# The tail of a cached-attention decode kernel: the last 224 rows of W_down on seven DMA engines, the output weights in three loads, two score buffers, masks on GpSimd

## The chip, the cores and the metric

The kernel runs on one core of one Trainium2 chip. The metric is the device time of one execution, in microseconds (us). A trace covers one execution. Its "span" runs from the first to the last instruction and is about 2 us shorter than the device time (658.7 against 660.76 us for the traced execution of the kernel before).

Engine names in the profile: PE is TensorE (PEld its weight loads), DVE is VectorE, ACT is ScalarE, POOL is GpSimd, SP is the engine that issues most DMAs. The core has 16 DMA engines, which all its queues share. An "instruction fetch" below is a packet that the trace marks as kind `instruction`; I read it as an engine fetching the next block of its program.

## The reference, cut to what matters

```python
# x: (2,1,512)   k_cache, v_cache: (2,32,8192,128)   wq: (512,4096)   wo: (4096,512)
# W_gate, W_up: (512,1376)   W_down: (1376,512)      all bfloat16
def _A_ref(x, k_cache, v_cache, wq, wo):            # one query token, 32 heads
    q = (x @ wq)...                                  # per head
    scores = einsum("bhqd,bhkd->bhqk", q, k) * Dh**-0.5
    o = softmax(scores) @ v
    return o.reshape(B, Sq, Hq*Dh) @ wo
def _B_ref(x, W_gate, W_up, W_down):
    gate = x @ W_gate ; up = x @ W_up
    return (relu(gate) * up) @ W_down
h  = x + _A_ref(layernorm(x), ...)
h2 = h + _B_ref(layernorm(h), ...)
```

K and V are 268 MB of the 281 MB that one execution reads. Four heads of one batch row are one step (8.4 MB of K and as much of V), so there are 16 steps.

## The kernel before: the parts that matter here

Every engine runs its own instruction list. A small helper records which operation wrote and read each named piece of data and emits the semaphore waits that this needs. VectorE multiplies K by the query and adds up (`products`, `sums`), ScalarE takes exponentials (`exps`), TensorE multiplies by V. One score buffer `sc` serves all steps, so the sum of step n waits until TensorE has finished step n-1:

```python
    def sums(n, lo, hi, key):
        red(sc[:, lo:hi], kt[n % 2][:, lo:hi, 0:8], AXIS.X, keys, [key])
    ...
    for n in range(L):
        if n:
            for k in ("sc", "pm"):
                s.last.pop(k, None)
                s.readers[k] = [v_done(n - 1)]
        scores(n, HALVES if n == 0 else (0, T))
```

At the end the weights come in on the SP queue in this order: `wo` (two loads of 2 MB), W_gate, W_up (three quarters, then one quarter), W_down (three loads, then the last 96 rows on 96 partitions):

```python
    for k in range(NGR):                                   # wo: 2 x 2 MB
        s.dma("sp", f"dwo{k}", ... writes=[f"wo{k}"], extra=[v_done(L - 1)])
    ...
    for f, r in blocks:                                    # W_down: 512, 512, 256 rows
        s.dma("sp", f"dwd{f}", ... writes=[f"wd{f}"], extra=x_free)
    s.dma("sp", "dwdl", lambda: sync.dma_start(out=wd_l, in_=B_W_down[FULL:F, :]),
          writes=["wdl"], extra=x_free)                    # the last 96 rows
```

and the tail computes

```python
    attention_rows(0, NK - JG, True)      # 16 matmuls with the first half of wo
    normalize(B - 1, NGR - 1)
    attention_rows(NK - JG, NK, False)    # 16 matmuls, wait for the whole second half
    # transpose on VectorE, layernorm, 12 gate matmuls, 12 up matmuls, product on VectorE (qrep),
    # columns of the product, 44 y matmuls, cast of y (sc), two output DMAs
```

The softmax here doesn't subtract the row's maximum and nothing guards it: scores larger than these inputs give would overflow.

## Time and profile before

| | before |
|---|---|
| time, median of 3 | 660.43 us (660.39 to 660.52) |
| span of the trace | 658.7 us |
| VectorE busy | 618.0 us, 94% |
| DMA, mean over the span | 427 GB/s, 281 MB read |
| VectorE waiting for K, in all | 4.6 us |

These are two rows of the page's second part, the span in 40 equal slices. The DMA row is the busy share of the 16 engines in tenths; the other is what they moved.

```profile
DMA  9999999999999999999999999999999999999996
GB/s 378 447 446 414 418 446 442 446 438 394 446 442 442 442 402 438 442 442 442 410 430 442 442 442 414 426 442 442 442 434 406 446 442 438 438 406 442 418 421 248
```

The DMA engines are busy from the first slice into the last one. The trace's packet records show the same from near: a packet of 65,536 bytes takes 2.42 us, and V arrives every 38.70 us, which is 16 such packets. So the length of the byte stream sets the time up to about 644 us. What can still change is how the last weights arrive and what is computed on them. This is the chain that ended last (start us, length us, what), in the kernel before:

```profile
621.36 22.94 DMA v<-in_A_wo_dram
644.29 0.14 issue
644.43 1.91 PE mm L596 x13
646.36 0.73 DVE osb L611
648.55 1.76 PE o L654 x12
650.72 1.85 PE mm L654 x12
652.66 0.69 DVE qrep L674
654.12 1.37 PE y L645 x44
655.51 0.29 DVE sc L711
```

The second load of `wo` lands at 644.29. Then come its matmuls, the transpose (osb), the gate matmuls (o), the up matmuls (mm), their product (qrep), the y matmuls and the cast. Nothing in this chain after 644.43 waits for a DMA.

The trace holds more: for each load, one landing time for each DMA engine that carried it. I sorted these and subtracted the start of the span. Each row of the next table is one load, and its 16 numbers are the 16 engines from first to last. The record does not say which engine a time belongs to.

```
kernel before, us            first 12 engines ............................................ 13th   14th   15th   last
wo, 2nd half  641.99 642.01 642.13 642.14 642.17 642.29 642.30 642.33 642.37 642.38 642.44 642.59 642.91 643.70 643.76 644.29
gate          645.30 645.32 645.44 645.45 645.48 645.60 645.61 645.65 645.68 645.69 645.76 645.89 646.23 647.00 647.08 647.61
up, 3/4       647.81 647.83 647.95 647.96 647.98 648.10 648.12 648.14 648.18 648.18 648.25 648.39 648.72 649.51 649.58 650.09
W_down, last  652.28 652.36 652.45 652.48 652.50 652.54 652.60 652.62 652.70 652.73 652.82 652.97 653.18 653.93 653.99 654.60
```

A load is usable when its last engine is done. Twelve engines finish within 0.6 us of each other, and four trail by up to 2.3 us. They fell back where instruction fetches came into the stream. The packet records show these: 16,384 bytes at 27.1 and 635.0 us, and 8,192 bytes at 177.2, 198.9 and 638.6 us. The loads that land between them show one step for each fetch.

### The profile page before, as it was taken

What the parts mean: (1) busy time and instruction counts of PE and PEld (TensorE: products, weight loads), DVE (VectorE), ACT (ScalarE), POOL (GpSimd) and SP (SyncE); (2) the same over time, 40 slices, a digit from 0 to 9 for tenths busy, and PEclk for the clock granted to TensorE, in tenths of its full rate; (3) what the DMA queues carried; (4) which work ended last, traced back from release to release, by engine and by line L of the source; (5) the groups of instructions that cost most, each with busy time, mean ns of one, the idle gap of its engine ahead of it and who ended that gap; (6) DMA issues with size and microseconds to landing.
All of it is one profiled execution on the core that took longest, in us unless ns stands there. A gap on an engine that the chain in (4) does not pass through costs nothing. (4 is left out here: it accounts for less than half of the span.)

```text
span 658.7 us, 3100 instructions
## 1 busy us (share of the span) xinstructions
PE 115.0 (17%) x1234; PEld 47.3 (7%) x1234; DVE 618.0 (94%) x184; ACT 59.4 (9%) x155; POOL 3.8 (1%) x15
## 2 busy tenths in 40 slices
PE   2200302003030110303011030300203030020365
PEld 1000100001010000101000010100001010010122
DVE  1799999999999999999999999999999999999972
ACT  2301010010101001010100101010010101001100
POOL 2000000000000000000000000000000000000000
PEclk9655655656565575656557565565756556575655
DMA  9999999999999999999999999999999999999996
GB/s 378 447 446 414 418 446 442 446 438 394 446 442 442 442 402 438 442 442 442 410 430 442 442 442 414 426 442 442 442 434 406 446 442 438 438 406 442 418 421 248
DMA packets 6474, 281.13 MB, mean 427 GB/s; under 512 B 738, under 2 KB 836, under 8 KB 1348
## 3 DMA queue, kind: packets, MB, share of 16 engines
q1 hardware_dynamic: 6456, 281.06, 98.9%
q8 instruction: 3, 0.05, 0.0%
q14 instruction: 3, 0.02, 0.0%
q10 hardware_dynamic: 12, 0.00, 0.0%
HBM read 281.05 MB, written 0.00 MB: 427 GB/s over the span
## 5 line engine op out<-in xcount | busy, mean ns | idle before, releaser
L364 DVE TENSOR_TENSOR k<-k,qrep 128x32768 bf16<-128x32768 bf16 (+3 forms) x18 | 275.9, 15327 | 4.6 <-DMA k<-in_A_k_cache_dram 4.6
L370 DVE TENSOR_TENSOR k<-k 128x4096 bf16<-128x4096 bf16 (+6 forms) x72 | 267.4, 3714 | 2.5
L406 PE MATMUL o<-v,pm 128*32 128x512 bf16 x960 | 83.9, 526 | 466.9 <-PEq L434 466.9
L383 ACT ACTIVATE pm<-sc 32x256 bf16<-32x256 f32 (+2 forms) x68 | 48.2, 709 | 562.9 <-DVE sc L227 562.1
L406 PEld LDWEIGHTS o<-v,pm 128*32 128x32 bf16 x960 | 35.2, 127 | 515.3 <-issue 508.4
L227 DVE TENSOR_REDUCE sc<-k 128x256 f32<-128x2048 bf16 (+2 forms) x17 | 36.7, 2160 | 0.8 <-PE o L406 0.3
L453 DVE TENSOR_REDUCE osb<-om 128x128 f32<-128x512 f32 x16 | 16.5, 1029 | 0.6
L383 ACT ACTIVATION_READ_ACCUMULATOR pm<-sc 32x1 f32 x68 | 15.8, 233 | 0.0
L349 DVE CAST qrep<-mm 32x512 bf16<-32x512 f32 x4 | 2.8, 696 | 11.1 <-PE mm L333 11.1
L449 DVE TENSOR_TENSOR om<-o,turn_of 128x512 f32<-128x512 f32 x16 | 10.9, 681 | 1.8 <-PE o L406 1.8
L413 PE MATMUL rep<-osb,spread 128*32 128x128 f32 x40 | 3.9, 420 | 48.4 <-DVE osb L453 45.0
L406 PE MATMUL o<-k,pm 128*32 128x512 bf16 x64 | 7.4, 628 | 7.7 <-ACT pm L383 5.3
L333 PE MATMUL mm<-v,om 128*64 128x512 bf16 x32 | 6.6, 572 | 8.7 <-DMA v<-in_A_wq_dram 8.5
L346 ACT ACTIVATE qrep<-mm 32x512 bf16<-32x512 f32 x12 | 7.0, 587 | 9.1 <-PE mm L333 8.9
L611 DVE STREAM_TRANSPOSE osb<-mm 128x512 f32<-128x512 f32 x1 | 0.7, 717 | 6.7 <-PE mm L596 6.7
L413 PEld LDWEIGHTS rep<-osb,spread 128*32 128x32 f32 x40 | 1.4, 146 | 50.9 <-DVE osb L453 46.6
L596 PE MATMUL mm<-v 128*2 128x512 bf16 x32 | 3.7, 620 | 3.0 <-DMA v<-in_A_wo_dram 3.0
L522 POOL TENSOR_TENSOR zm<-zm,zx 128x1 f32<-128x1 f32 x1 | 0.2, 191 | 627.5 <-ACT pm L383 627.5
L333 PEld LDWEIGHTS mm<-v,om 128*64 128x64 bf16 x32 | 2.5, 152 | 12.4 <-issue 10.3
L406 PEld LDWEIGHTS o<-k,pm 128*32 128x32 bf16 x64 | 2.0, 133 | 12.7 <-ACT pm L383 6.7
L301 DVE COPY xc<-st 128x8 f32<-128x8 f32 x1 | 0.2, 165 | 2.6 <-PE st L296 2.6
L654 PE MATMUL o<-k,sc 128*32 128x512 bf16 x12 | 1.9, 628 | 0.0
(81 smaller groups left out, 33.3 us busy)
## 6 DMA issues: line engine op xcount, KB each, us to landing
k<-in_A_k_cache_dram SPq DMA_DIRECT2D x2, 4096.0 KB, 26.8
v<-in_A_wq_dram SPq DMA_DIRECT2D x1, 4096.0 KB, 12.3
k<-in_A_v_cache_dram SPq DMA_DIRECT2D x1, 4096.0 KB, 31.4
v<-in_A_wo_dram SPq DMA_DIRECT2D x2, 2048.0 KB, 20.4
k<-in_A_v_cache_dram SPq DMA_DIRECT2D x1, 3072.0 KB, 38.3
k<-in_B_W_gate_dram SPq DMA_DIRECT2D x1, 1376.0 KB, 14.9
k<-in_B_W_up_dram SPq DMA_DIRECT2D x1, 1032.0 KB, 17.1
k<-in_A_v_cache_dram SPq DMA_DIRECT2D x1, 1024.0 KB, 40.4
```

Source lines behind the costliest of these rows:

```text
L227: s.op("dve", lambda: dve.tensor_reduce(out=out_, in_=in_, axis=axis, op=ALU.add), reads=reads, writes=writes)
L333: last = pe.matmul(out=ps[h * B * Q:(h + 1) * B * Q], lhsT=xnb[:, c].rearrange("p b q -> p (b q)"), rhs=wq_h[:, c, g:g + QP, h0 + h, :], s ...
L346: s.op("act", lambda src=src, dst=dst: act.activation(out=dst, in_=src, func=ACT.Copy), reads=[f"mm{t}"], writes=[key])
L349: s.op("dve", lambda src=src, dst=dst: dve.tensor_copy(dst, src), reads=[f"mm{t}"], writes=[key])
L364: s.op("dve", lambda: dve.tensor_tensor(out=kp, in0=kp, in1=_view(qrep[:, b, i, :], 0, [[0, hi - lo], [1, Dh]]), op=ALU.mult), reads=keys ...
L370: s.op("dve", lambda half=half, width=width: dve.tensor_tensor(out=kp[:, :, 0:half], in0=kp[:, :, 0:half], in1=kp[:, :, half:width], op=AL ...
L383: last = act.activation(out=p_of[ps, lo // TG:hi // TG, :, h], in_=sc[ps, lo:hi].rearrange("p (g t) -> p g t", t=TG), func=ACT.Exp, accum_ ...
L406: last = pe.matmul(out=o[g:g + W2], lhsT=pm[:, t // TG, :], rhs=vs[:, t:t + TG, :].rearrange("p t d -> p (t d)"), start=(t < P // Q * TG), ...
L413: return pe.matmul(out=rep_ps[u * Q:(u + 1) * Q, :], lhsT=spread.rearrange("k h m -> k (h m)"), rhs=osb[:, u, :], start=True, stop=True, s ...
L449: s.op("dve", lambda: dve.tensor_tensor(out=om.rearrange("p (t d) -> p t d", d=Dh), in0=o.rearrange("p (t d) -> p t d", d=Dh), in1=_view(t ...
L453: fn = lambda: dve.tensor_reduce(out=osb[:, u, :], in_=om.rearrange("p (t d) -> p d t", d=Dh), axis=AXIS.X, op=ALU.add)
L596: last = pe.matmul(out=ar_ps[g:g + B], lhsT=oc[:, k, :], rhs=wo_sb[:, k, :], start=False, stop=(k + P // Q >= NK), skip_group_check=True)
```

## The change

The intent: shift bytes of W_down from nine DMA engines to seven, so that the engines that end last have less to do; let half of the second `wo` matmuls run before the last of `wo` has landed; free VectorE's score sums from a wait; take three small mask reductions off VectorE. The diff, cut to its core (`...` marks cuts):

```diff
-    NF = F // P                      # 10 blocks of 128 rows, 96 rows left
+    NE = 7
+    NF = (F - 32 * NE) // P          # 9 blocks, 224 rows left
...
-    sc = sbuf("sc", (P, T), f32)
+    sc2 = [sbuf(f"sc{u}", (P, T), f32) for u in range(2)]
-    x_row = sbuf("x_row", (B, D), bf16)
+    x_row = osb.rearrange("p u d -> p (u d)")[0:B, 0:D // 2].bitcast(bf16)   # room; loaded again late
...
+        implied = [self.clock.get(t, {}) for t in out.items()]               # drop implied waits
+        out = {k: v for k, v in out.items() if all(c.get(k, 0) < v for c in implied)}
...
+    for h in range(G):               # three masks by GpSimd copies and memsets
+        s.op("pool", lambda q=q: pool.tensor_copy(eye_of[q], ident[q, q]), ...)
+        s.op("pool", ... pool.memset(head_blk[...]))
-        red(head_blk, ...)           # were three VectorE reductions
-        red(row_of[:, 0:B], ...)
-        red(eye_of, ...)
...
-            for k in ("sc", "pm"):
-                s.last.pop(k, None)
-                s.readers[k] = [v_done(n - 1)]
+            s.last.pop("pm", None)
+            s.readers["pm"] = [v_done(n - 1)]
...
-    for k in range(NGR):
+    WO = ((0, 0, JG), (1, 0, JG // 2), (1, JG // 2, JG))
+    for k, lo, hi in WO:             # wo: 2 MB, 1 MB, 1 MB
...
-    s.dma("sp", "dwdl", ... in_=B_W_down[FULL:F, :])
+    s.op("pool", lambda: pool.memset(X[0:Q, at:at + 4 * D], 0.0), writes=["wdl"], extra=x_free)
+    rest = B_W_down[FULL:F, :].rearrange("(h e i r) n -> h i e (r n)", h=2, e=NE, r=4)
+    for h in range(2):
+        for m in range(4):           # eight loads, seven partitions of 4 KB each
+            s.dma("act", f"dwl{h}{m}", lambda h=h, m=m: act.dma_start(
+                out=X[h * Q + m:h * Q + m + 4 * NE:4, at:at + 4 * D], in_=rest[h, m]), ...)
...
-    attention_rows(0, NK - JG, True)
     normalize(B - 1, NGR - 1)
-    attention_rows(NK - JG, NK, False)
+    for k, lo, hi in WO:
+        attention_rows(k * JG + lo, k * JG + hi, k == lo == 0)
...
-    s.op("pe", lambda: y_rows(act_t[0:LASTW, NF, :], wd_l, last=True), ...)      # 4 matmuls
+        for r in range(4):                                                       # 16 matmuls
+            last = y_rows(act_t[0:ML, NF + r, :], wd_l[:, r, :], last=(r == 3))
```

The cut leaves out one more edit: two of the four normalisations on VectorE are merged into one instruction.

There are 52 y matmuls instead of 44. The earlier blocks lose four with the tenth block, and the rest gains twelve.

More of the change, by code (lines that the diff above doesn't have):

```diff
@@ L69, in op @@
     def op(self, eng, fn, reads=(), writes=(), extra=(), gives=None, token=None):
+        if eng == "pool" and self.count[eng]:
+            extra = list(extra) + [(eng, self.count[eng])]
         waits = self.needs(eng, reads, writes, extra)
@@ L126 @@
     f32 = mybir.dt.float32
-    NF = F // P
-    FC = (F + P - 1) // P
+    NE = 7
+    NF = (F - 32 * NE) // P
+    FC = NF + 4
     FULL = NF * P
-    LASTW = F - FULL
+    ML = 32 + 4 * NE
     Q = P // G
@@ L149 @@
     assert Sq == 1 and Hkv == Hq and D == KC * P and Hq % (2 * G) == 0 and T % 32 == 0 and P == Dh
-    assert NQ % NS == 0 and P == 4 * Q and D == MT
+    assert F == FULL + 32 * NE and NQ % NS == 0 and P == 4 * Q and D == MT
     ctx.enter_context(tc.tile_critical(no_gpsimd_drain=True))
@@ L194 @@
     zi = late[:, NK + B * NQ:NK + B * NQ + B * NGR]
-    hd = sc[:, P // 2:P].bitcast(bf16).rearrange("p (c k b) -> p c k b", k=NR, b=B)
+    hd = sc2[0][:, P // 2:P].bitcast(bf16).rearrange("p (c k b) -> p c k b", k=NR, b=B)
     r2 = late[:, 2 * NK - 1:2 * NK]
+    x_late = vt.rearrange("p t d -> p (t d)")[0:B, NK * D + 4 * P:NK * D + 4 * P + D]
     act_t = late[:, 2 * NK:2 * NK + FC * B // 2].bitcast(bf16).rearrange("p (f b) -> p f b", b=B)
@@ L222 @@
     s.op("pool", lambda: pool.memset(pm, 0.0), writes=["pm"])
-    s.op("pool", lambda: pool.memset(osb, 0.0), writes=["osb"])
-    s.lists["pool"].append(((), lambda: pool.sem_inc(s.sem("o_in"), 1), None))
     def red(out_, in_, axis, reads, writes):
@@ L228, in red @@
              reads=reads, writes=writes)
+    for h in range(G):
+        q = slice(h * Q, (h + 1) * Q)
+        s.op("pool", lambda q=q: pool.tensor_copy(eye_of[q], ident[q, q]), reads=["ident"],
+             writes=["eye"])
+        s.op("pool", lambda h=h: pool.memset(head_blk[:, h:h + 1], 0.0), writes=[f"head{h}"])
+        s.op("pool", lambda h=h, q=q: pool.memset(head_blk[q, h:h + 1], 1.0),
+             writes=["head", f"head{h}"])
+    s.op("pool", lambda: pool.tensor_copy(row_of[:, 0:B], eye_of[:, 0:B]), reads=["eye"],
+         writes=["row_of"])
     def build_masks():
@@ L234, in build_masks @@
             i, ["lane"])
-        red(head_blk, ident.rearrange("p (h m) -> p h m", h=G), AXIS.X, i, ["head"])
-        red(row_of[:, 0:B], ident.rearrange("p (g q) -> p q g", q=Q)[:, 0:B, :], AXIS.X, i,
-            ["row_of"])
-        red(eye_of, ident.rearrange("p (g q) -> p q g", q=Q), AXIS.X, i, ["eye"])
         red(pick, ident.rearrange("p (h m) -> p m h", m=M4), AXIS.X, i, ["pick"])
@@ L300 @@
     s.op("pe", columns_of_x, reads=["x_row", "ident"], writes=["st"])
+    s.op("pool", lambda: pool.memset(osb, 0.0), writes=["osb"], extra=[s.last["st"]])
+    s.lists["pool"].append(((), lambda: pool.sem_inc(s.sem("o_in"), 1), None))
     s.op("dve", lambda: dve.tensor_copy(xc, x_ps), reads=["st"], writes=["xc"])
@@ L376, in sums @@
         keys = [f"k{n % 2}{x}" for x in "abc"]
-        red(sc[:, lo:hi], kt[n % 2][:, lo:hi, 0:8], AXIS.X, keys, [key])
+        red(sc2[n % 2][:, lo:hi], kt[n % 2][:, lo:hi, 0:8], AXIS.X, keys, [key])
     def exps(n, lo, hi, z, zkey, key, first=True):
@@ L383, in fn @@
                 last = act.activation(out=p_of[ps, lo // TG:hi // TG, :, h],
-                                      in_=sc[ps, lo:hi].rearrange("p (g t) -> p g t", t=TG),
+                                      in_=sc2[n % 2][ps, lo:hi].rearrange("p (g t) -> p g t", t=TG),
                                       func=ACT.Exp, accum_out=z[ps], scale=SCALE)
@@ L397, in scores @@
             products(n, lo, hi)
-        sums(n, 0, T, "sc")
-        exps(n, 0, T, zm[:, b, i:i + 1], "zm", "sc")
+        sums(n, 0, T, f"sc{n % 2}")
+        exps(n, 0, T, zm[:, b, i:i + 1], "zm", f"sc{n % 2}")
     def v_matmuls(vs, o, lo, hi):
@@ L500 @@
     wo_sb = vt.rearrange("p t d -> p (t d)")[:, 0:NK * D].rearrange("p (k n) -> p k n", n=D)
-    for k in ("sc", "pm", "va", "vb", "vc"):
-        s.last.pop(k, None)
-        s.readers[k] = [v_done(L - 1)]
-    for k in range(NGR):
+    s.last.pop("pm", None)
+    s.readers["pm"] = [v_done(L - 1)]
+    WO = ((0, 0, JG), (1, 0, JG // 2), (1, JG // 2, JG))
+    for k, lo, hi in WO:
         r0 = k * NS * G * Dh
-        s.dma("sp", f"dwo{k}", lambda k=k, r0=r0: sync.dma_start(
-            out=wo_sb[:, k * JG:(k + 1) * JG, :].rearrange("p k n -> p (k n)"),
-            in_=A_wo[r0:r0 + NS * G * Dh, :].rearrange("(p j) n -> p (j n)", p=P)),
-            writes=[f"wo{k}"], extra=[v_done(L - 1)])
+        s.dma("sp", f"dwo{k}_{lo}", lambda k=k, lo=lo, hi=hi, r0=r0: sync.dma_start(
+            out=wo_sb[:, k * JG + lo:k * JG + hi, :].rearrange("p k n -> p (k n)"),
+            in_=A_wo[r0:r0 + NS * G * Dh, :].rearrange("(p j) n -> p j n", p=P)[:, lo:hi, :]
+            .rearrange("p j n -> p (j n)")),
+            writes=[f"wo{k}_{lo}"], extra=[v_done(L - 1)])
+    s.dma("act", "dx2", lambda: act.dma_start(out=x_late, in_=A_x.rearrange("b s d -> (b s) d")),
+          writes=["x_late"], extra=[v_done(L - 1)])
     X = kt[L % 2].rearrange("p t d -> p (t d)")
     b, i = divmod(L, NQ)
-    for lo, hi, z, zkey, key in ((0, LATE, zm[:, b, i:i + 1], "zm", "sc0"),
-                                 (LATE, T, zx, "zx", "sc1")):
+    for lo, hi, z, zkey, key in ((0, LATE, zm[:, b, i:i + 1], "zm", "sca"),
+                                 (LATE, T, zx, "zx", "scb")):
         products(L, lo, hi)
-        if lo == 0:
-            s.readers["sc0"] = list(s.readers.get("sc", []))
-            s.readers["sc1"] = list(s.readers.get("sc", []))
-        red(sc[:, lo:hi], kt[L % 2][:, lo:hi, 0:8], AXIS.X, [f"k{L % 2}{x}" for x in "abc"], [key])
+        sums(L, lo, hi, key)
         exps(L, lo, hi, z, zkey, key)
-    x_free = [s.last["sc1"]]
-    s.op("pool", lambda: pool.tensor_tensor(out=zm[:, b, i:i + 1], in0=zm[:, b, i:i + 1], in1=zx,
-                                            op=ALU.add), reads=["zm", "zx"], writes=["zm"])
+    x_free = [s.last["scb"]]
+    zl = zm[:, b, i:i + 1]
+    s.op("pool", lambda: pool.tensor_tensor(out=zl, in0=zl, in1=zx, op=ALU.add), reads=["zm", "zx"], writes=["zm"])
     wgu = X[:, 0:2 * KC * F].rearrange("p (g c n) -> p g c n", c=KC, n=F)
@@ L529 @@
     at += NF * D
-    wd_l = X[0:LASTW, at:at + D]
+    wd_l = X[0:ML, at:at + 4 * D].rearrange("p (r n) -> p r n", n=D)
     blocks = [(f, min(4, NF - f)) for f in range(0, NF, 4)]
@@ L542 @@
             writes=[f"wd{f}"], extra=x_free)
-    s.dma("sp", "dwdl", lambda: sync.dma_start(out=wd_l, in_=B_W_down[FULL:F, :]),
-          writes=["wdl"], extra=x_free)
+    s.op("pool", lambda: pool.memset(X[0:Q, at:at + 4 * D], 0.0), writes=["wdl"], extra=x_free)
+    rest = B_W_down[FULL:F, :].rearrange("(h e i r) n -> h i e (r n)", h=2, e=NE, r=4)
+    cleared = s.last["wdl"]
+    for h in range(2):
+        for m in range(4):
+            s.dma("act", f"dwl{h}{m}", lambda h=h, m=m: act.dma_start(
+                out=X[h * Q + m:h * Q + m + 4 * NE:4, at:at + 4 * D], in_=rest[h, m]),
+                writes=[f"wdl{h}{m}"], extra=x_free + [cleared])
     lanes(L - 1)
@@ L548 @@
         s.op("pe", lambda lo=lo, hi=hi: v_matmuls(vl, o_ps[1], lo, hi),
-             reads=["pmsc0" if hi <= LATE else "pmsc1"]
+             reads=["pmsca" if hi <= LATE else "pmscb"]
              + [f"k{(N - 2) % 2}{x}" for x in (parts(lo, hi) or ["b"])], writes=["o1"])
@@ L583 @@
     invert_z()
-    for g in range(B * NGR - 1):
-        normalize(*divmod(g, NGR))
+    s.op("dve", lambda: dve.tensor_tensor(
+        out=oc[:, :, 0].rearrange("p (k j) -> p k j", j=JG), in0=ou[:, 0],
+        in1=_view(zi, 0, [[1, NGR], [0, JG]]), op=ALU.mult),
+        reads=[f"ou{g}" for g in range(NGR)] + ["zi"], writes=[f"oc{k}" for k in range(NGR)])
+    for k in range(NGR - 1):
+        normalize(B - 1, k)
     ar_ps = mm_ps[0]
@@ L591, in fn @@
             if first:
-                pe.matmul(out=ar_ps, lhsT=ident[0:B, :], rhs=x_row, start=True, stop=False,
+                pe.matmul(out=ar_ps, lhsT=ident[0:B, :], rhs=x_late, start=True, stop=False,
                           skip_group_check=True)
@@ L598, in fn @@
             return last
-        s.op("pe", fn, reads=["x_row", "ident", f"oc{k0 // JG}", f"wo{k0 // JG}"], writes=["mm0"])
+        s.op("pe", fn, reads=["x_late", "ident", f"oc{k0 // JG}", f"wo{k0 // JG}_{k0 % JG}"],
+             writes=["mm0"])
     gather(B * NGR - 1)
-    attention_rows(0, NK - JG, True)
     normalize(B - 1, NGR - 1)
-    attention_rows(NK - JG, NK, False)
+    for k, lo, hi in WO:
+        attention_rows(k * JG + lo, k * JG + hi, k == lo == 0)
     NB = D // Q
@@ L677 @@
     act_ps = sm_ps[:, 32:32 + FC * B].rearrange("p (f b) -> p f b", b=B)
-    actl_ps = rep_ps[0:LASTW, 32:32 + B]
+    actl_ps = rep_ps[0:ML, 32:32 + 4 * B].rearrange("p (r b) -> p r b", b=B)
     sel = ident[0:RW].rearrange("k (j q) -> k j q", q=Q)
@@ L686, in columns_of_act, with columns_of_rest @@
                       rhs=sel[:, 0:NBL, 0:B], start=True, stop=True, skip_group_check=True)
-        for f in range(4 * NBL, FC):
-            w = P if f < NF else LASTW
-            f0, r = blocks[NBL] if f < NF else (NF, 1)
-            c0 = f0 * P - offs[NBL] + f - f0
-            last = pe.matmul(out=act_ps[:, f] if f < NF else actl_ps, lhsT=actr[0:RW, c0:c0 + (w - 1) * r + 1:r],
-                             rhs=sel[:, NBL, 0:B], start=True, stop=True, skip_group_check=True)
-        return last
-    s.op("pe", columns_of_act, reads=["act", "ident"], writes=["sm", "rep"])
+        for f0, w in blocks[NBL:]:
+            for f in range(f0, f0 + w):
+                c0 = f0 * P - offs[NBL] + f - f0
+                last = pe.matmul(out=act_ps[:, f], lhsT=actr[0:RW, c0:c0 + (P - 1) * w + 1:w],
+                                 rhs=sel[:, NBL, 0:B], start=True, stop=True,
+                                 skip_group_check=True)
+        return last
+    def columns_of_rest():
+        for h, m in ((0, Q), (1, 4 * NE)):
+            for r in range(4):
+                c0 = FULL - offs[NBL] + 4 * h * 4 * NE + r
+                last = pe.matmul(out=actl_ps[h * Q:h * Q + m, r],
+                                 lhsT=actr[0:RW, c0:c0 + 4 * (m - 1) + 1:4],
+                                 rhs=sel[:, NBL, 0:B], start=True, stop=True,
+                                 skip_group_check=True)
+        return last
+    s.op("pe", columns_of_act, reads=["act", "ident"], writes=["sm"])
+    s.op("pe", columns_of_rest, reads=["act", "ident"], writes=["rep"])
     s.op("act", lambda: act.activation(out=act_t[:, 0:NF], in_=act_ps[:, 0:NF], func=ACT.Copy),
          reads=["sm"], writes=["act_t"])
-    s.op("dve", lambda: dve.tensor_copy(act_t[0:LASTW, NF], actl_ps),
-         reads=["rep"], writes=["act_l"])
+    s.op("dve", lambda: dve.tensor_copy(act_t[0:ML, NF:FC], actl_ps), reads=["rep"],
+         writes=["act_l"])
     for f0, r in blocks:
@@ L707, with rest_of_y @@
         s.op("pe", fn, reads=["act_t", f"wd{f0}"], writes=["y"])
-    s.op("pe", lambda: y_rows(act_t[0:LASTW, NF, :], wd_l, last=True), reads=["act_l", "wdl"],
-         writes=["y"])
-    y_row = sc[:, 0:P // 2].bitcast(bf16)
+    def rest_of_y():
+        for r in range(4):
+            last = y_rows(act_t[0:ML, NF + r, :], wd_l[:, r, :], last=(r == 3))
+        return last
+    s.op("pe", rest_of_y, reads=["act_l", "wdl"] + [f"wdl{h}{i}" for h in range(2)
+                                                    for i in range(4)], writes=["y"])
+    y_row = sc2[0][:, 0:P // 2].bitcast(bf16)
     s.op("dve", lambda: dve.tensor_copy(y_row, y_ps), reads=["y"], writes=["xnb"])
```

## The prediction

> **What bounds the kernel.** The DMA stream. In the slices of the page the DMA row is 9 to the end (427 GB/s), and the DMA records show each engine's packets back to back: a 65,536-byte packet takes 2.42 us and the V-cache landings repeat every 38.70 us, exactly 16 packets. VectorE (94% busy) only keeps pace: it waited 4.6 us in all for K (the waits). So until about 644 us nothing but bytes counts, and the bytes do not change. The last 15 us count. The chain that ended last goes: wo DMA (22.94 us, its last engine lands at 644.30), 13 to 16 matmuls (1.9 us), transpose, gate matmuls from 648.55, up matmuls from 650.72, y matmuls 654.12 to 655.49, output.
>
> The landing records hold one time per DMA engine. At the second half of wo twelve engines land from 641.98 to 642.6, one at 642.9, three late at 643.70 to 644.30. The late ones are those that carried the 16 KB and 8 KB instruction fetches (at 27, 177, 199, 635 and 639 us). The last W_down rows land at 654.60, before the last four y matmuls want them (about 655.1).
>
> **What the change does.**
> - wo in two pieces: 8 of 16 matmuls wait for the last landing, -0.93 us there. Its 8 KB packets (313 ns against 613 for 16 KB) add about 0.1 us to all later landings. But gate (lands 647.6) and the first part of up (650.1) are next: with +0.1 and the usual 0.13 us from landing to matmul, gate can start 0.6 us and up about 0.4 us earlier. So about 0.4 us survives.
> - W_down rest: eight DMAs with seven partitions each. The Trainium skill, "DMA: Bandwidth & Descriptors", "Why a DMA increments its semaphore by 16 and not by 1", says such a DMA runs on the lowest seven engines; no run here shows it yet. Those get 8 packets of 4 KB (159 ns each, +1.3 us, alternating with the SP queue's packets); the nine others lose about 0.5 us of W_down. If the late engines are among the nine, the wo, gate and up landings hold; if the alternation costs double (instruction fetches lengthened the stream by 1.2 to 2 times their own length) or a late engine is among the seven, they land 0.3 to 1.3 us later. W_down was not last, so its earlier tail buys nothing. Price: eight more y matmuls at 30 ns, +0.24 us; seven more small column matmuls, mostly under ScalarE's copy, +0.05.
> - GpSimd memset (32x2048, estimated 1.8 us from the 128x2048 one) and eight issues of 0.4 us end near 641: in time.
> - Two score buffers: remove VectorE's 0.25 us wait at 620.8; DMA-bound there, no gain.
> - Masks on GpSimd: about 1 us of VectorE before 7 us, while wq lands at 13.2: no gain.
> - Merged normalisation, fewer waits: -0.05 us.
>
> Sum: -0.4 + 0.24 + 0.05 - 0.05, about -0.15 us.
>
> **Prediction.** 660.3 us, 80% range 659.4 to 661.2. Faster by over 2%: 0.5%; within 2%: 98.5%; slower: 1%.
>
> **What would show it.** Eight matmuls (about 0.95 us) after the last wo landing; a small wait for gate or up before their matmuls, named as DMA; 52 y matmuls in about 1.6 us without a wait for W_down; seven engines landing wo, gate and up over 1.2 us later than before while the latest stays near 644.4; the V landings still 38.70 us apart; VectorE's first product still near 22.9 us.
>
> **What would make it wrong.** A late engine among the seven; costlier alternation of the two queues; instruction fetches that move to other times or engines because instruction counts change (each is worth up to 1.2 us on one engine); the up landing binding more or less than I count.

## More of the kernel before

```
kernel before                     engines that trail the pack: us behind the first engine
K, landing at  22.4 us            none (all 16 within 0.51)
after the fetch at  27.1 us       1.74
after the fetch at 177.2 us       1.34 1.74
after the fetch at 198.9 us       0.99 1.36 1.75
after the fetch at 635.0 us       0.91 1.33 1.70 1.75     (first half of wo)
after the fetch at 638.6 us       0.92 1.71 1.77 2.30     (second half of wo)
```

Each row is the next landing after the fetch. The times carry no engine number, so I match them by size. At the last step three lags hardly change, and the one at 1.33, by its size the engine of the fetch at 177.2 us, falls to 2.30. That fetch itself took 0.325 us, and the 16 KB packet it met took 1.273 us instead of 0.613.

## The result, and the profile after

| | before | after |
|---|---|---|
| time, median of 6 (same rounds) | 660.40 us (660.03 to 660.52) | 661.02 us (660.78 to 661.57) |
| ratio | | 1.0011 (95%: 0.9998 to 1.0024) |
| span of the trace | 658.7 us | 659.2 us |
| output DMAs issued at | 655.83 us | 655.98 us |
| from there to the end | 2.91 us | 3.20 us |

Ratios here and below are the mean time of one kernel's runs over the mean of the other's in the same rounds, so they are not quite the ratio of the medians quoted. The interval includes 1. A second set of five runs, beside two other kernels on one chip (below), again put the kernel after above: 660.93 against 660.51 us. So the change costs about half a microsecond, or nothing that a 95% interval can tell from zero.

The DMA and GB/s rows of the kernel after, for comparison with those above:

```profile
DMA  9999999999999999999999999999999999999995
GB/s 382 442 445 433 402 441 441 445 445 398 434 441 442 441 426 414 441 441 445 433 406 441 441 441 441 406 433 441 441 445 426 410 441 441 445 433 406 428 418 237
```

The body is unchanged: V still lands every 38.70 us, and VectorE waits 4.8 us for K in all. The chain that ended last, in the kernel after, last part:

```profile
632.92 17.66 DMA k<-in_B_W_up_dram
650.58 0.04 issue
650.62 1.92 PE mm L676 x12
652.63 0.69 DVE qrep L696
653.97 1.68 PE y L667 x47
655.66 0.29 DVE sc L750
```

The last DMA of the chain is no longer `wo` but the first part of W_up, landing at 650.58. From there the chain goes back to the issue of that load and through all of VectorE's work, which is why this page's summary gives 74% to DVE. That is only the path back through what released the load, not a new bound. The next lines, of the timeline around the tail of the kernel after (start, length, engine, line, operation, operands, in brackets the idle time before and what ended it), show where the gain from `wo` went:

```profile
634.38 1.79 POOL L554 MEMSET k<- 32x2048 bf16 x1
636.20 6.12 ACTq L559 DMA_DIRECT2D k<-in_B_W_down_dram  x8
644.31 1.02 PE L617 MATMUL mm<-v 128*2 128x512 bf16 x8 [1.75 <-DMA v<-in_A_wo_dram]
645.39 0.72 DVE L633 STREAM_TRANSPOSE osb<-mm 128x512 f32<-128x512 f32 x1 [5.86 <-PE mm L617]
648.21 1.89 PE L676 MATMUL o<-k,sc 128*32 128x512 bf16 x12 [0.64 <-DMA k<-in_B_W_gate_dram]
650.62 0.14 PEld L676 LDWEIGHTS mm<-k,sc 128*32 128x32 bf16 x6 [0.20 <-DMA k<-in_B_W_up_dram]
653.97 1.65 PE L667 MATMUL y<-k,v 128*2 128x128 bf16 x52
```

Only eight matmuls run after the last piece of `wo`, and the transpose starts at 645.39 instead of 646.36, 0.97 us earlier. But the gate matmuls now wait 0.64 us for their weights and the up matmuls wait again. Up starts at 650.62 instead of 650.72: of 0.97 us, 0.10 is left. The eight more y matmuls take that and more.

The landing table of the kernel after, made like the one above, shows why gate and up are late:

```
kernel after, us  first seven engines ........................... then nine ..................................................... last
wo, 3rd piece 642.15 642.22 642.25 642.29 642.30 642.33 642.47 642.53 642.55 642.65 642.72 643.24 643.39 643.84 643.91 644.27
gate          645.48 645.56 645.57 645.61 645.61 645.65 645.79 646.44 646.50 646.58 646.68 647.17 647.20 647.23 647.36 648.07
up, 3/4       647.97 648.06 648.07 648.10 648.11 648.15 648.29 649.10 649.17 649.24 649.35 649.68 649.69 649.72 649.86 650.58
```

The `wo` rows end alike (644.29 and 644.27). In the gate row only seven engines are still early. Seven have been held up by the rest of W_down, and the last one lands 0.46 us later than in the kernel before. Two suspicions follow. One: trailing engines are among the seven. The count says so: twelve engines do not trail, and if all seven that carry the rest were of these, five would still be early. Seven are, so two of the seven trail. Two: other changes are mixed in, because the fetch of 8 KB at 638.6 us is gone in the kernel after (there is none between 198.6 us and the end), which should by itself have made the last engine earlier. The last DMA engine and the last 0.29 us of the program needed experiments.

### The profile page after: what moved, and what is told of

It is laid out like the page before. It is cut to its first block, busy times and chain, and to the rows that moved or that the text cites. A ratio compares the mean times of both kernels' runs of the same rounds, so it can differ in the third digit from the quotient of the medians.

```text
span 659.2 us, 3135 instructions
## 1 busy us (share of the span) xinstructions
PE 115.5 (18%) x1248; PEld 47.5 (7%) x1248; DVE 617.4 (94%) x180; ACT 59.4 (9%) x155; POOL 7.7 (1%) x29
## 4 chain that ended last, share of the span: by engine, by line
DVE 74%; DMA 25%; PE 1%; issue 1%; SPq 0%; ACT 0%; DVEq 0%
DVE k L376 34%; DVE k L382 33%; DMA k<-in_A_k_cache_dram 22%; DVE sc L231 5%; DMA k<-in_B_W_up_dram 3%; DVE osb L465 1%; DVE om L461 1%; PE mm L676 0%; PE y L667 0%; DVE qrep L696 0%; SPq L285 0%; SPq L545 0%; PE sm L706 0%; DVE sc L750 0%; DVE ou L231 0%
```

## The experiments

There were eleven runs: eight kernels, then the kernel after and two of the eight once more. All were correct. Times are medians, in three batches, each with the kernel before in the same rounds. Every 95% interval includes 1, so the timings only rank. The reasons rest on the traces.

| run | runs | time us | before, same rounds | ratio (95%) |
|---|---|---|---|---|
| e1_wo | 5 | 660.37 | 660.59 | 0.9997 (0.9983 to 1.001) |
| e2_norest | 5 | 660.06 | 660.59 | 0.9992 (0.9978 to 1.0006) |
| e3_dvemasks | 5 | 660.53 | 660.59 | 1.0 (0.9986 to 1.0013) |
| e4_masks | 5 | 660.25 | 660.59 | 0.9996 (0.9982 to 1.0009) |
| e5_sc2 | 4 | 660.03 | 660.39 | 0.9992 (0.9977 to 1.0007) |
| e6_restsp | 4 | 660.73 | 660.39 | 1.0002 (0.9987 to 1.0018) |
| e7_rest | 4 | 661.29 | 660.39 | 1.0015 (0.9999 to 1.003) |
| e8_tuned | 5 | 659.64 | 660.39 | 0.999 (0.9976 to 1.0004) |
| r1_after | 5 | 660.93 | 660.51 | 1.001 (0.9996 to 1.0023) |
| r2_tuned | 5 | 659.88 | 660.51 | 0.9991 (0.9977 to 1.0004) |
| r3_wo | 5 | 660.26 | 660.51 | 0.9997 (0.9984 to 1.0011) |

And this is what each trace shows of the tail, in us from the start of the span: the last engine's landing of three loads, when the output was issued, how long it was from there to the end, and when the last 8 KB instruction fetch began. "VectorE records" counts VectorE's entries in the trace, waits and register instructions included.

```
             wo last   gate    up 3/4   output issued  to end   8 KB fetch   VectorE records
before        644.29   647.61   650.09      655.83       2.91      638.6          212
after         644.27   648.07   650.58      655.98       3.20      end            193
e1_wo         644.30   647.61   650.15      655.36       2.92      638.4          212
e2_norest     644.11   647.43   649.91      655.16       3.25      end            193
e3_dvemasks   644.24   648.04   650.54      655.97       2.83      653.8          196
e4_masks      644.31   647.62   650.13      655.25       2.91      638.4          209
e5_sc2        643.94   647.26   649.75      655.47       2.92      653.4          197
e6_restsp     644.49   647.80   650.38      656.00       3.34      end            193
e7_rest       644.79   648.98   651.48      656.37       2.86      638.6          212
e8_tuned      643.72   647.03   649.53      654.75       2.92      656.7          195
r1_after      644.09   647.78   650.28      655.70       3.20      end            193
r2_tuned      644.20   647.51   650.02      655.25       2.92      657.2          195
r3_wo         644.21   647.52   650.01      655.31       2.93      638.1          212
```

("end" means that it began 0.3 to 0.6 us after the last instruction. e3 and e7 have one more 8 KB fetch, 1.4 and 1.0 us after the last instruction, and after and r1 have one more, 1.3 us after it.) Three kernels were traced twice, and the output issue of the same kernel moved by 0.28, 0.50 and 0.05 us. A difference of up to 0.5 us between two single traces therefore proves nothing by itself. The 0.50 us, between e8_tuned and r2_tuned, has a cause that the landings show: the 16 KB fetch near 635 us set its engine back by about 1.5 us in both, but that engine was one of the early ones in e8_tuned, and one already 0.7 us behind in r2_tuned. The last engine then trailed by 1.6 us in one and 2.2 in the other.

A number that does not move with the whole stream is the lag of the last engine behind the first, here for gate:

```
                                              lag of the last engine, gate, us
8 KB fetch near 638 us, no rest before gate   before 2.31, e1_wo 2.20, e4_masks 2.29, r3_wo 1.99
neither                                       e2_norest 2.18, e5_sc2 1.95, e6_restsp 1.75, e8_tuned 1.63, r2_tuned 2.24
rest before gate, no such fetch               after 2.60, e3_dvemasks 2.68, r1_after 2.33
both                                          e7_rest 3.40
```

The rest adds 0.6 us (mean 2.53 against 1.95), and these two groups do not overlap. The fetch adds 0.2 us on average (2.20 against 1.95), and these two do overlap.

The TensorE clock is part of that. It is half of full speed in nearly all of the tail, but some executions get a stretch of 3.4 us at full speed. e4, e3, e7, r1 and r2 had one after 640 us.

### e1_wo: the kernel before, with only the `wo` split

```diff
-    for k in range(NGR):
+    WO = ((0, 0, JG), (1, 0, JG // 2), (1, JG // 2, JG))
+    for k, lo, hi in WO:
...
-    attention_rows(0, NK - JG, True)
     normalize(B - 1, NGR - 1)
-    attention_rows(NK - JG, NK, False)
+    for k, lo, hi in WO:
+        attention_rows(k * JG + lo, k * JG + hi, k == lo == 0)
```

> The kernel before with only the second half of wo loaded and used in two pieces. Theory T (the split works, but gate and up bind next): the transpose starts near 645.4 us instead of 646.36, gate and the first part of up land at most 0.1 us later than before (647.7 and 650.2), up starts near 650.3 instead of 650.72, the 44 y matmuls end near 655.1, total 0.3 to 0.4 us below before. Rival R1 (the split is worthless because the landings of gate and up already bound the kernel before): within 0.1 us of before.

The chain of e1_wo:

```profile
632.91 17.24 DMA k<-in_B_W_up_dram
650.20 1.92 PE mm L657 x12
652.21 0.69 DVE qrep L677
655.05 0.29 DVE sc L714
```

The transpose started at 645.42, gate landed at 647.61 and up at 650.15, and the up matmuls started at 650.20 instead of 650.72. The output went out 0.47 us earlier than before. Theory T holds, with a little more than its 0.3 to 0.4 us in the trace. The time fell by 0.2 us in both batches, less than the trace's 0.47 and inside the noise. Both traces of this kernel put the output at 655.3 to 655.4 us. The split is worth about half of the 0.93 us that it takes off its own wait, because the first part of W_up lands next.

### e2_norest: the kernel after, with W_down loaded as before

```diff
-    NE = 7
-    NF = (F - 32 * NE) // P
+    NF = F // P
...
-    for h in range(2):
-        for m in range(4):
-            s.dma("act", f"dwl{h}{m}", ...)
+    s.dma("sp", "dwdl", lambda: sync.dma_start(out=wd_l, in_=B_W_down[FULL:F, :]), ...)
```

> The kernel after with the last W_down rows put back as before (96 partitions, SP queue, 44 y matmuls), everything else as after. Theory T (the seven-engine rest costs: eight y matmuls, and it makes gate and up land about 0.5 us later because a late engine is among the seven): gate lands near 647.1 and the first part of up near 649.6, y ends near 654.7, the time is 0.7 to 1.0 us below after. Rival R1 (the rest costs only its eight y matmuls): 0.2 to 0.3 us below after, gate and up land as in after (648.07, 650.58).

The chain of e2_norest:

```profile
632.78 17.13 DMA k<-in_B_W_up_dram
649.96 1.92 PE mm L669 x11
651.97 0.69 DVE qrep L689
654.85 0.29 DVE sc L727
```

Up starts at 649.96 instead of 650.62 in the kernel after, 0.66 us earlier, and the output goes out 0.82 us earlier. So between these two traces the rest cost 0.66 us through the landings and 0.16 us through the added small matmuls and y matmuls, net. About 0.2 us of the 0.66 is a shift of the whole stream (the first engine landed gate at 645.48 against 645.25), and with the second trace of the kernel after, r1_after, the difference is 0.54 us at the output instead of 0.82. R1 (matmuls only) falls: the lag table puts every kernel with the rest before gate above every one without. The time was 0.5 us below the kernel before, while the kernel after was 0.6 above it in its own batch. The 3.25 us from output issue to end stayed.

### e7_rest: the kernel before, with only the seven-engine rest

This is the diff of e2_norest in the other direction, on the kernel before.

> The kernel before with only the seven-engine rest. Theory B (the engine of the 8 KB fetches at 177 and 638.6 us is one of the lowest seven, so fetch and rest add up on it): gate lands near 648.8 and the first part of up near 651.3, 1.2 us later than in before, the output is issued 1.2 to 1.5 us later (657.1 to 657.3), time about 661.8. Rival (the late engines are among the nine others, as my prediction hoped): gate lands at 647.6, up at 650.1, time 0.2 to 0.3 us above before.

The chain of e7_rest:

```profile
633.04 18.44 DMA k<-in_B_W_up_dram
651.53 1.84 PE mm L661 x10
656.05 0.29 DVE sc L734
```

And from its timeline, the y matmuls:

```profile
654.80 1.21 PE L652 MATMUL y<-k,v 128*2 128x128 bf16 x52
```

Gate landed at 648.98 and up at 651.48, 1.4 us later than in the kernel before. The eight small loads themselves show which kind of engine is to blame, since each has exactly seven landing times (an eighth update of its semaphore, at the issue, is left out):

```
e7_rest, us      seven engines of one load, first to last
3rd of eight   643.58 643.61 643.62 643.63 643.63 643.86 644.98
8th of eight   647.78 647.82 647.86 647.87 647.88 648.16 649.24
```

Five of the seven engines agree to 0.1 us, one is 0.3 us late and one more than 1 us late. Two of the trailing engines are among the seven. In this kernel the 8 KB fetch and the rest both sit on the later of the two and add up. Theory B holds for the landings. The output went out 0.54 us later than before, not the 1.2 to 1.5 us expected. Most of the difference is that this execution had its TensorE at full clock from 653.1 to 656.5 us: the 52 y matmuls took 1.21 us here and 1.65 us in the kernel after, and the up matmuls 1.84 instead of 1.92. Without that the output would have been about 1.06 us late (an estimate from these durations). The expectation also overlooked that in the kernel before up had landed 0.63 us before its matmuls started. The time (661.29, 0.9 us above before) is nearer to the expectation of 661.8 than the trace is.

### e6_restsp: the kernel after, with the rest last on the SP queue

```diff
-            s.dma("act", f"dwl{h}{m}", lambda h=h, m=m: act.dma_start(
+            s.dma("sp", f"dwl{h}{m}", lambda h=h, m=m: sync.dma_start(
```

> The kernel after with the eight seven-engine loads issued last on the SP queue instead of on the ACT queue. Theory T2 (of the 0.8 us that the rest cost, 0.6 us come from its packets going between those of wo, gate and up, on a late engine): gate lands near 647.4 and the first part of up near 649.9 as without the rest, y matmuls end near 655.1, output is issued 0.5 to 0.6 us earlier than in after (655.4). If instead the W_down tail then binds (the rest lands after 654.7) most of this is lost to a wait of the last 16 y matmuls. Rival (gate and up are late for another reason, such as the ACT queue or the memset): gate still lands at 648.07 or later.

The chain of e6_restsp, its end:

```profile
641.78 13.13 DMA k<-in_B_W_down_dram
654.91 0.14 issue
655.04 0.62 PE y L667 x16
655.69 0.29 DVE sc L750
```

The gate matmuls no longer wait; their weights landed at 647.80. But now the rest is last in line on the late engine and lands at 654.91, and the last 16 y matmuls wait for it. (In this execution the stream ran 0.4 us behind that of e2_norest; the last engine's `wo` landed at 644.49 against 644.11.) The output went out at 656.00, as in the kernel after. That is the alternative that the expectation named: issued early, the rest delays gate and up; issued late, it delays itself. Where the rest goes in the queue changes which wait one sees, not the sum on the late engine. The rest is alone at its end here, so its landings show its engines well: in the first of the eight loads, five engines land within 0.27 us, one 0.58 and one 1.08 us after the first. At gate, the four trailing engines of this trace were 0.63, 1.10, 1.34 and 1.75 us behind. By these sizes the two among the seven are those at 0.63 and 1.10, the ones that the 8 KB fetches at 199.2 and 177.6 us had set back.

### e3_dvemasks and e4_masks: the masks back on VectorE, and the masks alone

e3_dvemasks is the kernel after with the three reductions on VectorE again. e4_masks is the kernel before with the three masks made on GpSimd:

```diff
+    for h in range(G):
+        s.op("pool", lambda q=q: pool.tensor_copy(eye_of[q], ident[q, q]), ...)
+        ...
-        red(head_blk, ...)
-        red(row_of[:, 0:B], ...)
-        red(eye_of, ...)
```

> The kernel after with the three masks made on VectorE again. Theory F (the 8 KB instruction fetch that before had at 638.6 us belongs to VectorE's program, and having fewer VectorE instructions moved it past the end): the fetch comes back near 638.6 us on an engine that is already late and now also carries the rest, gate and up land 0.6 to 1.0 us later than in after, the time is 0.5 to 1.0 us above after. Rival: the fetch is another engine's, no fetch near 638.6 us, time within 0.2 us of after.

> The kernel before with only the masks moved to GpSimd. Theory F: the 8 KB instruction fetch at 638.6 us is gone, the last engine of the second half of wo lands near 643.8 instead of 644.30, gate and up land about 0.5 us earlier, the chain to the output is about 0.5 us shorter; the time is 0.1 to 0.5 us below before, the lower value if the fetch then delays the end of the program. Rival (the masks' move does nothing, as in my prediction): fetch stays, time within 0.1 us of before.

Theory F, that the masks' three instructions moved the 8 KB fetch away from 638.6 us, fell in both. In e4 the fetch stayed at 638.4 us and gate and up landed as before (647.62 and 650.13). In e3 it did not come back to 638.6 but to 653.8 us. The earlier output of e4 in its trace is no gain of the masks: the full clock came from 651.9 to 655.3 us, and with its y matmuls 0.27 and its up matmuls 0.28 us shorter than before, that is nearly all of the 0.58 us. Its median, 0.34 us below before, lies inside the interval. The y matmuls of e4:

```profile
653.81 1.07 PE L653 MATMUL y<-k,v 128*2 128x128 bf16 x44 [0.28 <-ACT v L704]
```

But e3 showed something else: with three more VectorE instructions than the kernel after, the time from output issue to end went back from 3.20 to 2.83 us, and the time was at the level of the kernel before. (Its TensorE, too, had a stretch at full clock, from 651.5 to 655.0 us, but its y matmuls then waited 0.19 us for W_down, and its output was issued when that of the kernel after was.)

### e5_sc2: the kernel before, with only the two score buffers

Only the two buffers, what makes room for them, and the pruning of implied waits; masks on VectorE, `wo` and W_down as before.

```diff
-    sc = sbuf("sc", (P, T), f32)
+    sc2 = [sbuf(f"sc{u}", (P, T), f32) for u in range(2)]
...
-            for k in ("sc", "pm"):
-                s.last.pop(k, None)
-                s.readers[k] = [v_done(n - 1)]
+            s.last.pop("pm", None)
+            s.readers["pm"] = [v_done(n - 1)]
```

> The kernel before with only the two score buffers (and what makes room for them: the x row kept in other storage and loaded again late; fewer waits). Theory S (the removed VectorE wait instructions, one for each score sum, move the 8 KB fetch of VectorE's program from 638.6 us to the end): no 8 KB fetch between 630 and 650 us; the last engine of the second half of wo lands near 644.1 instead of 644.30, up near 649.9 instead of 650.1; the chain starts 0.2 us earlier, but VectorE ends late in the last barrier and from output issue to end it takes 3.2 us instead of 2.9. Time within 0.3 us of before. Rival (the fetch follows the number of masks or the W_down split): fetch stays at 638.4 to 638.6.

This was half right. VectorE's list lost 15 records (197 instead of 212), the fetch left the sensitive place, and gate and up landed 0.34 us earlier. But it moved to 653.4 us, not to the end, and the end stayed normal at 2.92 us. Over all kernels in the table the fetch goes with the number of VectorE records: 209 to 212 records, 638 us; 197, 653.4; 196, 653.8; 195, 656.7 and 657.2; 193, the end. It begins when VectorE has started between 184 and 193 of its records. That this fetch is VectorE's own is the simplest reading; the trace does not label it, but the next run adds a sign of it.

### e8_tuned: W_down as before, two of the three masks back on VectorE

This is e2_norest plus two VectorE reductions, so that the fetch falls after the last W_down landing and before the end.

```diff
+        red(head_blk, ident.rearrange("p (h m) -> p h m", h=G), AXIS.X, i, ["head"])
+        red(row_of[:, 0:B], ident.rearrange("p (g q) -> p q g", q=Q)[:, 0:B, :], AXIS.X, i,
+            ["row_of"])
```

> The kernel after without the seven-engine rest (W_down as before) and with two of the three masks back on VectorE, so that VectorE's program fetch falls between the last W_down landing and the end. Theory: no fetch between 630 and 652 us, output issued near 655.2, output to end 2.9 us and not 3.25, span 658.0 to 658.1, time about 0.6 us below before and 0.3 us below the same kernel without these two instructions. Rival (the 0.33 us at the end is not tied to the fetch): output to end stays 3.2 us.

The chain of e8_tuned:

```profile
632.76 16.77 DMA k<-in_B_W_up_dram
649.57 1.92 PE mm L667 x8
654.43 0.29 DVE sc L725
```

The fetch fell at 656.7 us, and output to end was 2.92 us. The output was issued at 654.75, even 0.4 us earlier than expected, and the repetition gave 655.25. At 659.64 us it is the fastest kernel here: 0.75 us below before in the same rounds (0.63 in the repetition). That it beats e2_norest, 0.53 below before, is not shown: the two never ran in the same rounds. The 0.4 us are the luck with the 16 KB fetch told above.

What the two instructions did can be seen in VectorE's own records. In all six traces with 193 or 195 of them, VectorE pauses before record 192, a `DRAIN` of the program's end. The 8 KB fetch begins 0.5 to 0.8 us after that record:

```
            record 192 is the DRAIN      pause before it   it ends   8 KB fetch   output to end
after       in the last barrier               0.47         658.96      659.49        3.20
e2_norest   in the last barrier               0.47         658.19      658.73        3.25
e6_restsp   in the last barrier               0.47         659.13      659.94        3.34
r1_after    in the last barrier               0.47         658.68      659.21        3.20
e8_tuned    before the wait for the output    0.48         656.18      656.72        2.92
r2_tuned    before the wait for the output    0.48         656.69      657.22        2.92
```

In the seven other traces the same `DRAIN`s follow the record before them after 0.09 to 0.10 us. So the pause sits at one place in VectorE's list, whichever `DRAIN` stands there, and the fetch follows it. Two more instructions moved that place from the last barrier, where the others wait for VectorE, to a spot after which VectorE waits for the output in any case (1.01 us were left of that wait). The rival falls.

### r1_after, r2_tuned, r3_wo: three kernels once more, side by side

> The kernel after once more, beside the next two on one chip. If the account holds: 0.4 to 0.9 us above before; gate's last engine lands near 648.1, output issue to end 3.2 us.

> The kernel of the run e8_tuned once more. If the account holds: 0.5 to 0.9 us below before and 1.0 to 1.6 us below after; gate's last engine lands near 647.1 to 647.4, output issue to end 2.9 us. If its lead in the first batch was chance: within 0.2 us of before.

> The kernel of the run e1_wo once more: 0.2 to 0.5 us below before by the account.

On one chip in the same rounds the medians were 660.93 (after), 660.51 (before), 660.26 (`wo` split alone) and 659.88 (tuned). The five runs of after (660.73 to 661.43) and of tuned (659.63 to 660.25) do not overlap; both overlap with those of before (660.18 to 661.09). The order is repeated, and the sizes within what was expected for the times. Two landings missed their ranges: r1's gate at 647.78, 0.3 us earlier than expected, and r2's gate at 647.51, 0.1 us later.

## Why the prediction was right, and where it was wrong

The measured 661.02 us lies in the predicted range, 659.4 to 661.2, and "within 2%" was right. The expected sign was not: the sum was -0.15 us and the result is about +0.4 to +0.6. That the range held is owed to its width of 1.8 us, not to the reasoning: the term for the rest was taken as nothing and was 0.4 to 0.7 us, and the term for the end of the program was missing. Point by point:

- **"The DMA stream" bounds the kernel: right.** V lands every 38.70 us in both kernels, and VectorE's first product started at 22.90 instead of 22.94 us.
- **"8 of 16 matmuls wait for the last landing, -0.93 us there ... So about 0.4 us survives": right, for the split alone.** The transpose came 0.97 us earlier in the kernel after; in e1_wo 0.47 us survived to the output.
- **"If the late engines are among the nine, the wo, gate and up landings hold": this branch was the one my number used, and it is the step that failed.** Two trailing engines are among the seven (the count in the gate row of the kernel after, and the landing times of the rest in e7_rest and e6_restsp). The prediction named the other branch, "a late engine is among the seven, they land 0.3 to 1.3 us later", but did not weigh it in the sum. Gate and up landed 0.46 and 0.49 us later than before, and removing the rest made them 0.64 and 0.67 us earlier (e2_norest). Over all traces the rest adds 0.6 us to the lag of the last engine at gate.
- **"If the alternation costs double": it did not.** Four of the seven landed 0.96 to 1.20 us behind the first engine in the gate row of the kernel after, and 1.13 to 1.38 in the up row, near the +1.3 us of eight packets. The last of `wo` landed at 644.27, against 644.29 before and 644.11 in e2_norest. The aside that fetches cost "1.2 to 2 times their own length" was too low: by the matched lags, a 16 KB fetch set its engine back by about 1.5 us and an 8 KB one by 0.65 to 0.98, which is 1.4 to 3 times what the fetch took.
- **"W_down was not last, so its earlier tail buys nothing": right.** In no trace of the kernel before or of e1_wo do the y matmuls wait for W_down; in each of the two places where the rest was tried its traces have the output later than in the trace without it (e2_norest).
- **"+0.24 us" and "+0.05" for more matmuls: about right.** From qrep to the cast it was 2.85 us before and 3.03 after, +0.18: the y matmuls to the cast took 0.30 us more, and they started 0.12 us sooner after qrep.
- **"Two score buffers ... no gain" was right about the wait, and wrong about a side effect.** Fifteen fewer VectorE records moved an 8 KB fetch off a trailing DMA engine at 638.6 us. In e5_sc2 gate and up landed 0.34 us earlier. But the gain is not fixed: in e1_wo and e2_norest the last engine trails by 2.20 and 2.18 us with and without that fetch, since the engine of the 16 KB fetch near 635 us was then as late (2.20 and 2.17 at `wo`). On average it is 0.2 us, below what single traces resolve.
- **"Eight issues of 0.4 us end near 641": missed.** The GpSimd memset took 1.79 us, as estimated, but the eight issues on the ACT queue took 6.12 us, 0.77 each, and ended at 642.3. No run shows a cost of that.
- **"Merged normalisation, fewer waits: -0.05 us"** was not tested alone.
- **"Masks on GpSimd ... no gain": right for the masks alone** (e4_masks leaves the landings as they were). In the whole change they were the last VectorE instructions that put the fetch at the very end: 212 records less 15 (two buffers), 1 (merged normalisation) and 3 (masks) are the 193.
- **The end of the program was not in the sum.** From output issue to end it is 3.20 to 3.34 us in all four traces with 193 VectorE records and 2.83 to 2.93 us in the nine others. In the slow ones VectorE's drain is the last to arrive in the final barrier (at 658.85 us in the kernel after, all others by 658.57). It starts 0.47 us after the record before it, instead of 0.09. e8_tuned and e2_norest differ by two masks, and the 0.33 us went away, because the pause then falls before a wait (table at e8_tuned). The prediction's warning of "instruction fetches that move" was about the right thing at the wrong place.

Up to the output, the steps between single traces are -0.47 (split, e1_wo), -0.20 (all else but the rest, e2_norest against e1_wo) and +0.82 (rest, after against e2_norest), together +0.15 us. With +0.29 us at the end, that is the span's +0.44 us. This sum closes by construction, since each step starts where the last one ended; it is no test, and each step carries the 0.5 us by which single traces differ. Of the -0.20, 0.16 us is that the first engine landed gate earlier too (645.25 against 645.41), and I can tie that to no edit.

What stays open: what VectorE does in the pause before its record 192. The fetch record begins only after the pause, and in the four slow traces after the last instruction. So the two are tied by place and order, in six traces of four kernels, and not by a wait that the trace names. Around the fetch near 638 us no such pause is seen: in the kernel before, VectorE's records there follow one another within 0.04 us. And which physical engines trail was not identified, only that two of them are among the seven of such a load, by their lags those that the 8 KB fetches near 177 and 199 us had set back.

## What to carry to other kernels

When a DMA stream is the bound, a load is as late as its slowest engine: look at the landing times of each engine before moving bytes between engines, and check that the engines that get more are not those that trail. Taking half a microsecond off one wait is worth only the distance to the next landing. And in a kernel tuned to tenths of a percent, adding or removing a handful of instructions moves instruction fetches; here these moved the end by 0.3 us and one landing by up to 1 us, as much as the intended changes did.

## What the Trainium skill lacked or had wrong

- "DMA: Bandwidth & Descriptors", "Why a DMA increments its semaphore by 16 and not by 1": by its rule a DMA over seven partitions uses seven engines, the lowest-numbered ones. Nothing wrong here, but seven is not among the counts that it lists as seen. The traces agree on the count, seven landing times for each such load. They do not number the engines, so "lowest" is not shown here.
- The same page, "Latency and other measured facts", lists engines 7 and 15 as usually slower and ties that, as a best guess, to descriptor rings of the software path. Four engines trailed by 0.9 to 2.3 us at the second half of `wo`, one for each instruction fetch seen in the stream up to 635 us (one of them fell back by another 0.98 us at the 8 KB fetch at 638.6 us), and two of the trailing engines were among the seven of a seven-partition load. No page gives this cost of a fetch to the data stream.
- "Runtime: NRT & Kernel Launch", "Instruction fetch mechanics", says that instruction memory is refilled in 16 KiB blocks and that the cost is mostly hidden. The traces show blocks of 16,384 bytes and also of 8,192 bytes. The cost was not hidden from the load that shared the DMA engine (0.98 us at 638.6 us); and kernels in which an 8 KB fetch follows a pause of VectorE in the last barrier took 3.20 to 3.34 us from output issue to end instead of 2.83 to 2.93.
- "DMA: Bandwidth & Descriptors", "Issuing engines are not separate DMA queues", says that DMAs of different issuing engines interleave on the same 16 engines. Nothing wrong or lacking here; the traces agree: with the eight loads on the ACT queue, the engines that carried them fell about 1.0 to 1.2 us behind the others at gate, near the 1.3 us of the added packets themselves.
